# One chunk's x scaled ahead of a mask, one projection ordered by its low half, raw weights issued a round later, the last output tile in two halves

## The chip, the cores and the metric

The kernel runs on one core of a Trainium2 chip. The metric is the device time of one execution in microseconds (us). The core has five engines that work side by side and wait for one another through semaphores: TensorE (PE: matrix products; its weight loads are listed as PEld), VectorE (DVE), ScalarE (ACT), GpSimd (POOL) and SyncE (SP), which here only issues transfers. Each engine takes its instructions strictly in program order.

## The reference

Three layers follow one another. The first is attention with a decay: for each of 2 x 8 heads the 768 positions are taken in blocks of 64, and each block adds a masked product of its own q, k, v and a product with a running state of 64 x 64.

```python
for b in range(nb):                       # blocks of 64 positions
    intra = einsum('bhic,bhjc->bhij', qb, kb) * Dmask
    intra = einsum('bhij,bhjd->bhid', intra, vb)
    inter = einsum('bhid,bhde->bhie', qb * lam_pow, kv_state)
    out[:, :, sl] = intra + inter
    kv_state = lam_block * kv_state + einsum('bhsd,bhse->bhde', kb * rev_pow, vb)
```

Its output is x with 1536 tokens x 512 features. The second layer normalises each token (x divided by its root mean square, times a gain), forms silu(xn @ w_gate) * (xn @ w_val) with 1536 hidden features, and multiplies by w_out. The third takes the maximum of three products (768 features each) and multiplies by a last w_out. Activations are float32; the weights lie in memory as 64-bit floats.

## The kernel before, in words

**Numbers in two parts.** Every operand of the dense layers is held as a high half, rounded to the matrix engine's float32r, and a low half, the rest (names ending in h and l: xh, xl; wh, wl; hh, hl). A product is three matmuls: high x high, weight-high x operand-low, weight-low x operand-high (mm3, L467). A high half is made by ACT, its low half by POOL (DVE in a few places).

**Weights.** A unit is a 128 x 512 piece of a weight matrix. SP loads its raw 64-bit words (load_to, L152; three buffers). ACT takes two readings of the words (L238, L239), DVE does three steps (L196, L199, L202), POOL adds (L204); that gives float32 W. Then ACT rounds it to wh (L167) and POOL forms wl (L170). Three buffers of raw words mean that the load of raw unit n+3 waits until POOL's L204 of unit n is done.

**Attention.** The 1536 tokens are 12 chunks of 128. What one chunk needs is cut into pieces with one-letter names: T transposes k and q (L294, L296, copied to kT, qT by ACT), K scales the keys with the decay (kd, L284, POOL), C makes the scores and the state's products (sc, L318, L323), a and b apply the mask (A, L330, DVE; a also advances the state, S, L348), M mixes (px, L374) and reads px twice on ACT (squares sq, L385; x times the gain, L387), U sums the squares (pm on PE, ms on DVE, the power ri on POOL, L404), N spreads ri over a matrix (pb, L413), scales x with it on DVE (L415) and rounds it to xh on ACT (L417), R forms xl on POOL (L426). V finishes the state.

**The order of the work.** The table `orders` holds one string of letters for each round; in round s the letter T works on chunk s, C, a, b and V on s-1, M and U on s-2, N and R on s-3, K on s+1. This table is the order on every engine. Rounds 0 to 6 run ahead of the dense layers (the prologue, L972): in each, T of chunk s also asks for v of chunk s+1 and k, q of chunk s+2 (loads_to), then one raw unit is loaded (L987), and from round 2 on one unit is begun (begin_unit, L989: ACT's L238 and L239 go at the end of the round).

**Dense layers.** A block is 512 tokens, that is four chunks. The first stage's step 0 (hidden1, L605) makes pg = gate product, pv = value product of block 0: proj (L472) runs four slices of three matmuls each, and after every second slice gap() (L442) lets in the next pieces of attention and of weight making. The remaining attention pieces are spread over such gaps until about a quarter of the run. The last work is out2 (L847): twelve tiles of 128 tokens x 512 features, six matmuls each (L858 to L860), an addition on DVE (L865) and a store issued by SP (L868).

Of the kernel before, what the change touches and what calls it, by code (L numbers as in the profile page):

```python
# [12 lines left out]
ALU = mybir.AluOpType  # L13
# [5 lines left out]
P = 128  # L19
# [7 lines left out]
def tile_decay_attention_swiglu_maxout(  # L27
# [16 lines left out]
    nc = tc.nc  # L44
# [3 lines left out]
    KD = DM // P  # L48
    F1 = w_gate.shape[1] // P
    F2 = w1.shape[1] // P  # L50
    NB = 512
    HF = 2 * P
# [3 lines left out]
    NBLK = NT // NB  # L56
    CPB = S // P
    NCH = NT // P
    CPNB = NB // P
# [11 lines left out]
    def bank(name):  # L71
        return psum.tile([P, 512], F32, tag="bank", name=name)
# [70 lines left out]
    units = {}  # L143
# [6 lines left out]
    pos = {"load": 0, "made": 0, "raw": 0, "step": 0, "gap": 0, "quiet": False, "lag": 3, "narrow": True, "seam": False}  # L150

    def load_to(n):  # L152
        while pos["load"] < min(n, len(raw_list)):
            nm, f = raw_list[pos["load"]]
            t = wp.tile([P, KD, 2 * P], I32, tag="raw", name="wraw", bufs=3)
            for to, src in crosswise(t, source[nm](f)) if nm in "gv" else [(t, source[nm](f))]:
                nc.sync.dma_start(out=to, in_=src)
            raws[nm, f] = t
            pos["load"] += 1
# [260 lines left out]
    def rest(c):  # L420
# [7 lines left out]
    named = dict(M=(2, mixed), N=(3, normed), C=(1, scores), a=(1, masked(0)), R=(3, rest),  # L428
                 b=(1, masked(1)), U=(2, summed), V=(1, advance), T=(0, lambda c: (loads_to(c + 2), turn(c))),
                 K=(-1, decayed_keys))  # L430
    orders = ["MCaNbTURVK"] * (CPNB + 2) + ["MCaNRbTUVK"] + ["MNCRaUbVTK"] * NCH
    attn_q = [(s_, named[ch][1], s_ - named[ch][0]) for s_ in range(NCH + 3) for ch in orders[s_]
              if (ch == "K") <= s_ - named[ch][0] < NCH]
    gaps = [0, 0]
# [32 lines left out]
    def mm3(out, wh, wl, xh_, xl_, first, last):  # L467
        nc.tensor.matmul(out=out, lhsT=wh, rhs=xh_, start=first, stop=False)  # L468
        nc.tensor.matmul(out=out, lhsT=wh, rhs=xl_, start=False, stop=False)  # L469
        nc.tensor.matmul(out=out, lhsT=wl, rhs=xh_, start=False, stop=last)  # L470

    def proj(ps, unit, bh, bl):  # L472
        wh, wl = unit
        for kk in range(KD):
            ks = slice(kk * P, (kk + 1) * P)
            mm3(ps, wh[:, ks], wl[:, ks], bh[:, kk, :], bl[:, kk, :], kk == 0, kk == KD - 1)
            if kk % 2:
                gap()

    def split(dst_h, dst_l, src):  # L480
# [124 lines left out]
    def hidden1(f, j):  # L605
        bh, bl = x_block(j)
        pg = bank("pg")
        proj(pg, units["g", f], bh, bl)
        pv = bank("pv")
        proj(pv, units["v", f], bh, bl)  # L610
        if j == NBLK - 1:
            free(("g", f), ("v", f))
        sg = act.tile([P, NB], F32, tag="sg", name="sg", bufs=1)
        nc.scalar.activation(out=sg, in_=pg, func=AF.Silu)
        nc.vector.tensor_tensor(out=sg, in0=pv, in1=sg, op=ALU.mult)  # L615
        return sg
# [43 lines left out]
    def free(*keys):  # L660
        for key in keys:
            del units[key]
            room[held.pop(key)] += 1
# [183 lines left out]
    def out2(g, j, t):  # L847
        last = g == F2 // 2 - 1
        if g == 0 and t == 0:
            acc_sb[j] = act.tile([P, KD, NB], F32, tag="acc", name="acc_sb", bufs=3)  # L850
        ts = slice(t * P, (t + 1) * P)
        acc = bank("acc")
        for d in range(2):
            while ("p", 2 * g + d) not in units:
                third_of_unit()
            wh, wl = units["p", 2 * g + d]
            hh, hl = parts[j, d]
            nc.tensor.matmul(out=acc, lhsT=hh[:, ts], rhs=wh, start=d == 0, stop=False)  # L858
            nc.tensor.matmul(out=acc, lhsT=hh[:, ts], rhs=wl, start=False, stop=False)  # L859
            nc.tensor.matmul(out=acc, lhsT=hl[:, ts], rhs=wh, start=False, stop=d == 1)  # L860
        y = acc_sb[j][:, t, :]
        if g == 0:
            nc.scalar.copy(out=y, in_=acc)
        else:
            nc.vector.tensor_tensor(out=y, in0=acc, in1=y, op=ALU.add)  # L865
        if last:
            r0 = j * NB + t * P
            nc.sync.dma_start(out=out[r0:r0 + P, :], in_=y)  # L868
        if (j, t) == (NBLK - 1, NB // P - 1):
            free(("p", 2 * g), ("p", 2 * g + 1))  # L870
        gap()
        if t % 2 and g < 2:
            third_of_unit()
# [70 lines left out]
    with tc.manual_schedule():  # L944
        nc.scalar.dma_start(out=lam8, in_=lam.rearrange("(o h) -> o h", o=1).to_broadcast([P, H]))
        loads_to(0)
        for to, src in crosswise(g_sb, rms_g.rearrange("(a p) -> p a", p=P)):
            nc.scalar.dma_start(out=to, in_=src)
        make_identity(nc, ident)
        nc.vector.memset(ones, 1.0)  # L950
        nc.vector.memset(zeros, 0.0)
        nc.scalar.activation(out=mhalf, in_=zeros[:, 0:1], func=AF.Silu)
        nc.vector.memset(mhalf, -0.5)
        warm = bank("warm")
        for i in range(9):
            nc.tensor.matmul(out=warm[:, 0:P], lhsT=zeros, rhs=zeros, start=True, stop=True)
        nc.vector.tensor_tensor(out=diag, in0=ident[:, :C], in1=ident[:, C:], op=ALU.add)
        for h in range(H):
            nc.vector.tensor_tensor_scan(
                out=Tm[:, h, :], data0=lam8[:, h:h + 1].to_broadcast([P, C]), data1=diag,  # L960
                initial=0.0, op0=ALU.mult, op1=ALU.add)
        for hf in range(2):
            nc.vector.tensor_copy(out=lamh[64 * hf:64 * hf + 64, :],
                                  in_=lam8.rearrange("p (a t) -> p t a", t=2)[64 * hf:64 * hf + 64, hf, :])
        for a in range(NP):
            nc.vector.tensor_tensor_scan(
                out=lami[:, a, :], data0=lamh[:, a:a + 1].to_broadcast([P, C]), data1=zeros[:, :C],
                initial=1.0, op0=ALU.mult, op1=ALU.add)
        loads_to(1)
        pos["narrow"] = False  # L970
        unit_ = None
        for s_ in range(CPNB + 3):  # L972
            if stage1:
                unit_ = stage1.pop(0)
            while attn_q[0][0] == s_:
                fn = attn_q[0][1]
                attn_step()
                if unit_ and fn is named["b"][1]:
                    words_of_unit(0, *unit_)
                elif unit_ and fn is named["U"][1]:  # L980
                    words_of_unit(1, *unit_)
                    if stage2:
                        finish_unit(*stage2.pop(0))
                elif unit_ and fn is named["V"][1]:
                    words_of_unit(2, *unit_)
                    stage2.append(unit_[:3])
            load_to(pos["load"] + 1)  # L987
            if s_ > 1:
                begin_unit()  # L989
        pos["narrow"] = True  # L990
        finish = first_stage()
        pos["step"] = len(steps)
        second_stage(finish)
# [31 lines left out]
```

## Time and profile before

| | |
|---|---|
| median of 3 runs | 547.83 us (547.78 to 549.16) |
| the profiled execution | 550.31 us, its span 548.5 us |
| PE busy | 529.8 us (97% of the span) |
| DVE, ACT, POOL busy | 376.5, 278.6, 316.3 us |
| PE over the span's 40 slices | 7697979999... then 99% to the end |
| the last chain of waits, by engine | PE 85%, POOL 4%, issue 3%, DVE 3%, SP's queue 2%, ACT 2% |

The span is the time from the first to the last instruction; 550.31 - 548.5 = 1.8 us lie around it. A digit of the PE row is the busy share of 13.7 us in tenths. So PE has unfilled time only in the first seven or eight slices, some 100 us, in which attention, the making of weights and the first dense steps share the engines. "issue" in a row means that an engine waited for nothing that the profile shows. In a row of the time line the first number is the start, the second the time that the instructions took, and a bracket at the end is the idle time ahead of it and what ended that.

### The profile page before, as it was taken

How to read it: one execution, taken by the hardware profiler on the slowest of the kernel's cores; microseconds unless marked ns; L12 is line 12 of the kernel's file. 1: busy time of each engine (PE TensorE's matmuls, PEld its weight loads, DVE VectorE, ACT ScalarE, POOL GpSimd, SP SyncE). 2: the span in 40 equal slices, each digit the busy share in tenths (PEclk: the TensorE clock that was granted, in tenths of full speed). 3: DMA queues.
4: the chain of work that ended last, by engine and by line, in shares of the span. 5: the costliest groups of instructions: out<-in, count | busy, mean ns of one | idle time of the engine just before them, and what ended most of it. 6: DMA issues, size and time to landing. Idle time of an engine off the chain costs nothing.

```text
span 548.5 us, 9716 instructions
## 1 busy us (share of the span) xinstructions
PE 529.8 (97%) x3722; PEld 438.9 (80%) x3722; DVE 376.5 (69%) x663; ACT 278.6 (51%) x541; POOL 316.3 (58%) x251
## 2 busy tenths in 40 slices
PE   7697979999999999999999999999999999999997
PEld 7685858878888888888888888888888888888885
DVE  6688995447795666657776686877777477684464
ACT  3576754344556665255446426556466755651120
POOL 2469996212899557165455736986387554962050
PEclk9978999999999999999999999999999999999999
DMA  8987566000212222121221312121123222300014
GB/s 193 231 195 185 140 179 155 2 3 0 78 34 82 78 67 86 39 76 39 78 76 39 115 39 77 40 76 38 40 78 114 82 76 75 83 33 0 0 55 176
DMA packets 65454, 44.67 MB, mean 81 GB/s; under 512 B 40064, under 2 KB 61568, under 8 KB 65408
## 3 DMA queue, kind: packets, MB, share of 16 engines
q1 hardware_dynamic: 64704, 44.05, 28.3%
q8 instruction: 29, 0.48, 0.4%
q14 instruction: 17, 0.14, 0.1%
q10 hardware_dynamic: 704, 0.01, 0.1%
HBM read 40.90 MB, written 3.15 MB: 80 GB/s over the span
## 4 chain that ended last, share of the span: by engine, by line
PE 85%; POOL 4%; issue 3%; DVE 3%; SPq 2%; ACT 2%; DMA 1%; POOLq 0%; ACTq 0%
PE p L676 34%; PE r L676 8%; PE acc L468 6%; PE acc L470 6%; PE acc L469 6%; PE q L676 4%; PE acc L859 3%; PE acc L858 3%; PE acc L860 3%; PE pv L468 2%; PE pv L469 2%; PE pv L470 2%; PE pg L468 2%; SPq L92 2%; PE pg L470 2%
## 5 line engine op out<-in xcount | busy, mean ns | idle before, releaser
L170 POOL TENSOR_TENSOR wl<-W,wh 128x512 fp32r<-128x512 f32 x77 | 105.6, 1371 | 39.4 <-ACT wh L167 39.2
L204 POOL TENSOR_TENSOR W<-W,wraw 128x512 int32<-128x512 int32 x60 | 81.3, 1356 | 79.3 <-DVE W L202 70.8
L167 ACT CAST wh<-W 128x512 fp32r<-128x512 f32 x77 | 47.8, 621 | 85.3 <-POOL W L204 84.9
L482 POOL TENSOR_TENSOR hl<-sg,hh 128x512 fp32r<-128x512 f32 x36 | 48.5, 1348 | 25.7 <-ACT hh L481 25.7
L676 PE MATMUL p<-xh,wh 128*128 128x512 f32 x148 | 57.6, 389 | 0.0
L676 PE MATMUL p<-xl,wh 128*128 128x512 f32 x148 | 57.6, 389 | 0.0
L676 PE MATMUL p<-xh,wl 128*128 128x512 f32 x148 | 57.6, 389 | 0.0
L468 PE MATMUL acc<-hh,wh 128*128 128x512 f32 x144 | 56.5, 393 | 0.0
L469 PE MATMUL acc<-hl,wh 128*128 128x512 f32 x144 | 56.1, 389 | 0.0
L470 PE MATMUL acc<-hh,wl 128*128 128x512 f32 x144 | 56.1, 389 | 0.0
L831 DVE TENSOR_TENSOR acc_sb<-acc,acc_sb 128x512 f32<-128x512 f32 x46 | 31.8, 691 | 21.6 <-PE acc L470 20.6
L238 ACT ACTIVATE W<-wraw 128x512 f32<-128x512 f32 x60 | 40.2, 670 | 6.8 <-DMA wraw<-in_moe_w_dram 4.3
L481 ACT CAST hh<-sg 128x512 fp32r<-128x512 f32 x36 | 22.3, 620 | 35.0 <-DVE sg L615 26.4
L239 ACT ACTIVATE wraw<-wraw 128x512 int32<-128x512 uint32 x60 | 39.7, 662 | 0.0
L731 ACT COPY c<-p 128x512 f32<-128x512 f32 x34 | 20.0, 588 | 38.1 <-PE p L676 38.0
L482 POOL TENSOR_TENSOR hl<-m,hh 128x512 fp32r<-128x512 f32 x18 | 24.0, 1343 | 23.0 <-ACT hh L481 22.9
L196 DVE TENSOR_SCALAR mid<-W 128x512 f32<-128x512 f32 x50 | 34.2, 685 | 3.0 <-ACT W L238 3.0
L199 DVE TENSOR_SCALAR mid<-mid 128x512 int32<-128x512 int32 x50 | 34.7, 694 | 0.7
L676 PE MATMUL p<-yh,wh 128*128 128x512 f32 x90 | 35.0, 389 | 0.0
L676 PE MATMUL p<-yl,wh 128*128 128x512 f32 x90 | 35.0, 389 | 0.0
L676 PE MATMUL p<-yh,wl 128*128 128x512 f32 x90 | 35.0, 389 | 0.0
L202 DVE SCALAR_TENSOR_TENSOR W<-wraw,mid 128x512 int32<-128x512 int32 x50 | 34.0, 680 | 1.0
(175 smaller groups left out, 1349.1 us busy)
## 6 DMA issues: line engine op xcount, KB each, us to landing
wraw<-in_moe_w_out_dram SPq DMA_DIRECT2D x18, 512.0 KB, 3.4
wraw<-in_moe_w_dram SPq DMA_DIRECT2D x18, 512.0 KB, 3.6
kn<-in_k_dram SPq DMA_DIRECT2D x12, 256.0 KB, 4.3
qn<-in_q_dram SPq DMA_DIRECT2D x12, 256.0 KB, 5.3
vn<-in_v_dram SPq DMA_DIRECT2D x12, 256.0 KB, 4.2
wraw<-in_moe_w_gate_dram SPq DMA_DIRECT2D x12, 256.0 KB, 3.0
wraw<-in_moe_w_gate_dram SPq DMA_DIRECT2D x24, 128.0 KB, 3.6
wraw<-in_moe_w_val_dram SPq DMA_DIRECT2D x12, 256.0 KB, 3.0
```

Of the source, the lines that this page charges most:

```text
L167: nc.scalar.copy(out=wh, in_=W.bitcast(F32))
L170: nc.gpsimd.tensor_tensor(out=wl, in0=W.bitcast(F32), in1=wh.bitcast(F32), op=ALU.subtract)
L196: nc.vector.tensor_scalar(out=mid[key].bitcast(F32), in0=W.bitcast(F32), scalar1=LEAST, scalar2=MOST, op0=ALU.max, op1=ALU.min)
L199: nc.vector.tensor_scalar(out=mid[key], in0=mid[key], scalar1=0x07FFFFFF, scalar2=3, op0=ALU.bitwise_and, op1=ALU.logical_shift_left)
L204: nc.gpsimd.tensor_tensor(out=W, in0=W, in1=lo, op=ALU.add)
L238: nc.scalar.activation(out=W.bitcast(F32), in_=hi.bitcast(F32), func=AF.Abs)
L239: nc.scalar.activation(out=lo, in_=lo.bitcast(U32), func=AF.Copy, scale=2.0 ** -29)
L468: nc.tensor.matmul(out=out, lhsT=wh, rhs=xh_, start=first, stop=False)
L469: nc.tensor.matmul(out=out, lhsT=wh, rhs=xl_, start=False, stop=False)
L470: nc.tensor.matmul(out=out, lhsT=wl, rhs=xh_, start=False, stop=last)
L482: nc.gpsimd.tensor_tensor(out=dst_l, in0=src, in1=dst_h.bitcast(F32), op=ALU.subtract)
L676: nc.tensor.matmul(out=ps, lhsT=w[:, ks], rhs=r[:, o + k, :], start=first and k == 0 and n == 0, stop=k == 1 and n == 2, skip_group_check= ...
```

## The change

It has four parts. (1) In round 6 the order "MCaNRbTUVK" becomes "MCNRabTUVK": N of chunk 3 stands ahead of the mask a of chunk 5. (2) In step 0 the gate projection orders its twelve matmuls so that the eight that read xh come first and the four that read xl last; the gaps stay after the sixth and the twelfth. (3) No raw unit is loaded in round 0, so each of the prologue's raw loads is issued one round later. (4) The last of the twelve output tiles is computed as two halves of 256 columns, each in a bank of its own, with an addition and a store each.

On DVE, round 6 before and then after (x<-x,pb is L415 of chunk 3; A<-sc the two masks of chunk 5; W<-wraw,mid a step of weight making):

```order
49 L202 SCALAR_TENSOR_TENSOR W<-wraw,mid 128x512
50 L330 TENSOR_TENSOR A<-sc_826,Tm 128x4x64
51 L348 SCALAR_TENSOR_TENSOR S<-S,lami,sc_826 128x64 x4
52 L415 TENSOR_TENSOR x<-x,pb 128x512
53 L330 TENSOR_TENSOR A<-sc_827,Tm 128x4x64
54 L196 TENSOR_SCALAR mid<-W 128x512
```

```order
49 L202 SCALAR_TENSOR_TENSOR W<-wraw,mid 128x512
50 L415 TENSOR_TENSOR x<-x,pb 128x512
51 L330 TENSOR_TENSOR A<-sc_824,Tm 128x4x64
52 L348 SCALAR_TENSOR_TENSOR S<-S,lami,sc_824 128x64 x4
53 L330 TENSOR_TENSOR A<-sc_825,Tm 128x4x64
54 L196 TENSOR_SCALAR mid<-W 128x512
```

The scaling of x moves over one mask and four state instructions. No row of ACT or POOL moves against its neighbours.

On PE, the first half of the gate projection in step 0, before and then after (pg is its bank; px the mixing of chunk 5 in the first gap):

```order
353 L400 MATMUL pm<-ones,sq 128x1 x4
354 L468 MATMUL pg<-xh,wh 128x512
355 L469 MATMUL pg<-xl,wh 128x512
356 L470 MATMUL pg<-xh,wl 128x512
357 L468 MATMUL pg<-xh,wh 128x512
358 L469 MATMUL pg<-xl,wh 128x512
359 L470 MATMUL pg<-xh,wl 128x512
360 L374 MATMUL px_932<-qs,S 64x64
```

```order
353 L400 MATMUL pm<-ones,sq 128x1 x4
354 L478 MATMUL pg<-xh,wh 128x512
355 L478 MATMUL pg<-xh,wl 128x512
356 L478 MATMUL pg<-xh,wh 128x512
357 L478 MATMUL pg<-xh,wl 128x512
358 L478 MATMUL pg<-xh,wh 128x512
359 L478 MATMUL pg<-xh,wl 128x512
360 L374 MATMUL px_928<-qs,S 64x64
```

All readers of xl now stand behind the first gap, as the last four of the twelve.

On SP, the difference at the head of its queue (kn, qn, vn are loads of k, q, v; wraw a raw unit; rows with + are new there):

```order
+L92 DMA kn<-in_k_dram 128x8x64
+L92 DMA qn<-in_q_dram 128x8x64
+L92 DMA vn<-in_v_dram 128x8x64
 L92 DMA kn<-in_k_dram 128x8x64
 L92 DMA qn<-in_q_dram 128x8x64
```

```order
 L157 DMA wraw<-in_moe_w_out_dram 128x1024
-L92 DMA vn<-in_v_dram 128x8x64
-L92 DMA kn<-in_k_dram 128x8x64
-L92 DMA qn<-in_q_dram 128x8x64
 L157 DMA wraw<-in_moe_w_gate_dram 128x2x256
```

Three loads of 256 KB now go ahead of each of the first six raw units; behind the sixth the two orders agree again.

```diff
--- before.py
+++ after.py
@@ -428,7 +428,7 @@
     named = dict(M=(2, mixed), N=(3, normed), C=(1, scores), a=(1, masked(0)), R=(3, rest),
                  b=(1, masked(1)), U=(2, summed), V=(1, advance), T=(0, lambda c: (loads_to(c + 2), turn(c))),
                  K=(-1, decayed_keys))
-    orders = ["MCaNbTURVK"] * (CPNB + 2) + ["MCaNRbTUVK"] + ["MNCRaUbVTK"] * NCH
+    orders = ["MCaNbTURVK"] * (CPNB + 2) + ["MCNRabTUVK"] + ["MNCRaUbVTK"] * NCH
     attn_q = [(s_, named[ch][1], s_ - named[ch][0]) for s_ in range(NCH + 3) for ch in orders[s_]
               if (ch == "K") <= s_ - named[ch][0] < NCH]
     gaps = [0, 0]
@@ -469,12 +469,15 @@
         nc.tensor.matmul(out=out, lhsT=wh, rhs=xl_, start=False, stop=False)
         nc.tensor.matmul(out=out, lhsT=wl, rhs=xh_, start=False, stop=last)
 
-    def proj(ps, unit, bh, bl):
+    def proj(ps, unit, bh, bl, early=False):
         wh, wl = unit
-        for kk in range(KD):
-            ks = slice(kk * P, (kk + 1) * P)
-            mm3(ps, wh[:, ks], wl[:, ks], bh[:, kk, :], bl[:, kk, :], kk == 0, kk == KD - 1)
-            if kk % 2:
+        todo = [(kk, w, x) for kk in range(KD) for w, x in ((wh, bh), (wh, bl), (wl, bh))]
+        if early:
+            todo.sort(key=lambda e: e[2] is bl)
+        for n, (kk, w, x) in enumerate(todo):
+            nc.tensor.matmul(out=ps, lhsT=w[:, kk * P:(kk + 1) * P], rhs=x[:, kk, :], start=n == 0,
+                             stop=n == len(todo) - 1)
+            if n % 6 == 5:
                 gap()
 
     def split(dst_h, dst_l, src):
@@ -605,7 +608,7 @@
     def hidden1(f, j):
         bh, bl = x_block(j)
         pg = bank("pg")
-        proj(pg, units["g", f], bh, bl)
+        proj(pg, units["g", f], bh, bl, early=pos["step"] == 0)
         pv = bank("pv")
         proj(pv, units["v", f], bh, bl)
         if j == NBLK - 1:
@@ -850,22 +853,27 @@
             acc_sb[j] = act.tile([P, KD, NB], F32, tag="acc", name="acc_sb", bufs=3)
         ts = slice(t * P, (t + 1) * P)
         acc = bank("acc")
+        todo = []
         for d in range(2):
             while ("p", 2 * g + d) not in units:
                 third_of_unit()
             wh, wl = units["p", 2 * g + d]
             hh, hl = parts[j, d]
-            nc.tensor.matmul(out=acc, lhsT=hh[:, ts], rhs=wh, start=d == 0, stop=False)
-            nc.tensor.matmul(out=acc, lhsT=hh[:, ts], rhs=wl, start=False, stop=False)
-            nc.tensor.matmul(out=acc, lhsT=hl[:, ts], rhs=wh, start=False, stop=d == 1)
+            todo.extend(((hh, wh), (hh, wl), (hl, wh)))
         y = acc_sb[j][:, t, :]
-        if g == 0:
-            nc.scalar.copy(out=y, in_=acc)
-        else:
-            nc.vector.tensor_tensor(out=y, in0=acc, in1=y, op=ALU.add)
-        if last:
-            r0 = j * NB + t * P
-            nc.sync.dma_start(out=out[r0:r0 + P, :], in_=y)
+        r0 = j * NB + t * P
+        ends = last and (j, t) == (NBLK - 1, NB // P - 1)
+        for cs in (slice(0, HF), slice(HF, NB)) if ends else (slice(0, NB),):
+            if cs.start:
+                acc = bank("acc")
+            for n, (x, w) in enumerate(todo):
+                nc.tensor.matmul(out=acc[:, cs], lhsT=x[:, ts], rhs=w[:, cs], start=n == 0, stop=n == len(todo) - 1)
+            if g == 0:
+                nc.scalar.copy(out=y, in_=acc)
+            else:
+                nc.vector.tensor_tensor(out=y[:, cs], in0=acc[:, cs], in1=y[:, cs], op=ALU.add)
+            if last:
+                nc.sync.dma_start(out=out[r0:r0 + P, cs], in_=y[:, cs])
         if (j, t) == (NBLK - 1, NB // P - 1):
             free(("p", 2 * g), ("p", 2 * g + 1))
         gap()
@@ -984,7 +992,8 @@
                 elif unit_ and fn is named["V"][1]:
                     words_of_unit(2, *unit_)
                     stage2.append(unit_[:3])
-            load_to(pos["load"] + 1)
+            if s_:
+                load_to(pos["load"] + 1)
             if s_ > 1:
                 begin_unit()
         pos["narrow"] = True
```

## Rows read from the trace of the kernel before

**Rows 1.** Time line of PE, 18 to 80 us: instructions behind an idle time.

```profile
18.60 0.34 PE L323 MATMUL sc<-vn,kd 64*64 64x64 f32 x8 [1.24 <-issue]
...
25.92 0.69 PE L323 MATMUL sc<-vn,kd 64*64 64x64 f32 x29 [2.62 <-issue]
...
42.52 0.50 PE L468 MATMUL pg<-xh,wh 128*128 128x512 f32 x1 [1.01 <-ACT xh L417]
...
44.76 0.79 PE L469 MATMUL pg<-xl,wh 128*128 128x512 f32 x1 [1.74 <-POOL xl L426]
...
70.52 0.46 PE L374 MATMUL px<-qs,S 64*64 64x64 f32 x16 [0.94 <-DVE S L348]
...
75.97 0.32 PE L318 MATMUL sc<-qT,kT 64*64 64x64 f32 x2 [2.14 <-ACT x L387]
...
79.92 0.38 PE L400 MATMUL pm<-ones,ss 128*128 128x1 f32 x2 [0.70 <-ACT sg L614]
```

**Rows 2.** Time line of POOL, 38 to 48 us: four of its instructions.

```profile
38.18 0.55 POOL L404 TENSOR_TENSOR ri<-ms,mhalf 128x1 f32<-128x1 f32 x1 [1.91 <-DVE ms L402]
...
41.17 1.30 POOL L204 TENSOR_TENSOR W<-W,wraw 128x512 int32<-128x512 int32 x1
...
43.43 1.27 POOL L426 TENSOR_TENSOR xl<-x,xh 128x512 fp32r<-128x512 f32 x1
...
46.41 1.47 POOL L204 TENSOR_TENSOR W<-W,wraw 128x512 int32<-128x512 int32 x1
```

**Rows 3.** Time line of ACT, 15 to 48 us: four that waited.

```profile
15.60 0.67 ACT L238 ACTIVATE W<-wraw 128x512 f32<-128x512 f32 x1 [0.59 <-DMA wraw<-in_moe_w_gate_dram]
...
20.86 0.62 ACT L417 CAST xh<-x 128x512 fp32r<-128x512 f32 x1 [2.45 <-DVE x L415]
...
41.85 0.62 ACT L417 CAST xh<-x 128x512 fp32r<-128x512 f32 x1 [1.32 <-DVE x L415]
...
47.91 0.62 ACT L167 CAST wh<-W 128x512 fp32r<-128x512 f32 x1 [2.84 <-POOL W L204]
```

**Rows 4.** Time line of DVE, 39 to 44 us.

```profile
39.98 0.42 DVE L330 TENSOR_TENSOR A<-sc,Tm 128x256 f32<-128x256 f32 x1
...
41.08 0.68 DVE L415 TENSOR_TENSOR x<-x,pb 128x512 f32<-128x512 f32 x1
...
43.47 0.42 DVE L303 TENSOR_TENSOR qs<-pq,lami 128x256 f32<-128x256 f32 x1 [0.78 <-ACT qT L300]
```

**Rows 5.** Time line of SP: issues of loads, 9 to 15 us.

```profile
9.00 3.10 SPq L157 DMA_DIRECT2D wraw<-in_moe_w_gate_dram  x3
12.15 0.60 SPq L92 DMA_DIRECT2D vn<-in_v_dram  x1
...
15.21 2.98 SPq L157 DMA_DIRECT2D wraw<-in_moe_w_val_dram  x3
```

**Rows 6.** The page's engines and instruction queue (packets, MB, share); then 22.8 to 23.0 us.

```profile
PE 529.8 (97%) x3722; PEld 438.9 (80%) x3722; DVE 376.5 (69%) x663; ACT 278.6 (51%) x541; POOL 316.3 (58%) x251
...
q8 instruction: 29, 0.48, 0.4%
...
q8 instruction: 1, 0.02, 51.9%
```

**Rows 7.** Stretches: length, busy PE PEld DVE ACT POOL, granted clock, DMA share, GB/s.

```profile
27.00:31.00 4.00, 3.89 (x53) 3.69 (x51) 3.22 (x11) 2.49 (x5) 0.62 (x2) 0.54 0.74 186
31.00:34.00 3.00, 3.00 (x97) 2.88 (x98) 2.00 (x7) 2.45 (x8) 3.00 (x4) 0.50 1.05 250
```

**Rows 8.** The end: additions of the last tiles, a weight load elsewhere, the stores' landing.

```profile
543.61 0.69 DVE L865 TENSOR_TENSOR acc_sb<-acc,acc_sb 128x512 f32<-128x512 f32 x1 [0.67 <-PE acc L860]
544.97 0.69 DVE L865 TENSOR_TENSOR acc_sb<-acc,acc_sb 128x512 f32<-128x512 f32 x1 [0.67 <-PE acc L860]
...
14.06 0.97 PEld L400 LDWEIGHTS pm<-ones,sq 128*128 128x128 f32 x8
...
DMA to landing us min/median/max: 2.0/2.0/2.0
```

## The prediction

> **What bounds the kernel now.** I read the busy shares first, then PE's time line for what it waits for, then POOL, ACT and DVE around those waits. PE is busy 97% of the span [rows 6], so only the early part can give anything, and there I ask which engine ends each wait. PE has three kinds of idle time. Twice it stops in the middle of a run of equal matmuls, for 1.24 and 2.62 us, and the releaser is "issue", not a semaphore [rows 1]. At the start of step 0 it waits 1.01 us for xh of chunk 3 (ACT) and 1.74 us for its xl (POOL) [rows 1]. Between 70 and 80 us it waits 0.94 us for DVE, 2.14 and 0.70 us for ACT, 3.78 us in all [rows 1]; after 79.92 no wait of this size is left, and PE alone sets the end.
>
> The last group decides. From 38.18 us POOL works without a gap: ri, wl, xl, W (41.17), kd, xl (43.43), ri, wl, W (46.41); only the first row has a bracket [rows 2]. ACT, in order, stands 2.84 us until 47.91 for that W [rows 3], and the squares of chunk 5 are queued behind it; DVE's work on x comes behind those. So from 38 to 80 us a chain POOL, ACT, DVE carries the time, and PE meets it again at 70.5, 76.0 and 79.9. What PE gains between 42 and 70 us is lost at these waits unless the chain comes earlier too.
>
> **The change part by part.**
>
> N ahead of mask a. In round 6 the scaling of x starts at 41.08, behind the mask that starts at 39.98 and four state instructions [rows 4]; its matmul pb is done before. Moved in front it starts at 39.98, 1.10 us sooner. ACT is idle from 41.85 - 1.32 = 40.53 [rows 3], so xh is begun at about 40.7, not 41.85. PE's wait for it, 1.01 us, goes: PE came to it at 42.52 - 1.01 = 41.51 [rows 1], and its own work before that is late next. The mask and the state come 0.68 us later, but the products that read them run only in the first gap. On DVE the copy-dependent qs at 43.47 waited 0.78 us for ACT [rows 4]; ACT is about a microsecond ahead, so DVE's following work comes some 0.7 us sooner.
>
> Low half last. xl of chunk 3 comes from POOL at 43.43 + 1.27 = 44.70. POOL's order does not change and it has no gap since 38.18 [rows 2], so this time stands. Six matmuls that read xh now run ahead of it, about 1.4 us at 0.23 us each, then chunk 5's mixing in the gap; by then xl is there. PE's wait of 1.74 us goes. No instruction is added. Together PE is 1.01 + 1.74 = 2.75 us ahead at the end of the first projection. What is worth of that at the end: nothing, since ri, wl, W on POOL and all that ACT and DVE do behind them start when they did; the waits at 70 to 80 us grow from 3.78 us by the lead. Bounds for this term: 2.75 us gained (chain not binding), and 0.5 us lost or gained in it, because DVE's earlier work meets other POOL instructions: POOL's W took 1.47 us at 46.41 against 1.30 at 41.17 [rows 2], 0.17 us for each of about three such instructions. I take a gain of 0.2 us, near the lower end, since POOL's row at 46.41 has DVE beside it before and after.
>
> Raws a round later. Each of the first six raw units now stands behind three more loads of 256 KB. Before, raw unit 0 was issued at 9.00 and ACT waited for it, 0.59 us, until 15.60 [rows 3, 5]. The three loads took from 12.15 to 15.21, 3.06 us, to issue [rows 5], so unit 0 is 3.1 us later: ACT's reading at about 18.7. Queued behind it on ACT are the squares and x of chunk 1, then xh of chunk 0, before which ACT stood idle 2.45 us, until 20.86 [rows 3]. That cover takes 2.45 of 3.1; 0.6 us remain, on kT and qT of chunk 3 and so on PE's scores of chunk 3. They are hidden as long as PE stops 2.62 us, until 25.92, in those scores [rows 1]; without that stop they cost 0.6 us. k, q and v come about 3 us sooner, but no wait of PE in these rows is for them, so nothing is gained. From unit 3 on a raw load must wait for POOL's W three units back in either order, and k, q, v no longer queue behind that wait. I take 0, with ends of +0.6 (or what the next paragraph gives).
>
> The two stops. PE runs 2 x 3722 instructions, and a queue named instruction moved 29 packets in the span [rows 6]: one for about 257. The stops come one round apart, in the same product of the scores, and a packet of that queue started between 22.8 and 23.0 us [rows 6], 3 us before PE went on. I read the stops as waits for PE's own instructions behind a full load queue. [...] Whether the new order makes them shorter or longer the rows don't tell: bytes asked for by 27 us are about equal, in another sequence. I take 0. Ends: both stops gone, 3.86 us; a further one like the larger, 2.62 us more. [...]
>
> The last tile. Two additions start 544.97 - 543.61 = 1.36 us apart, so six matmuls of 512 columns take 1.36 us, 0.227 each [rows 8]. Twelve of 256 columns take 1.36 us again if the time goes by columns; if each also pays a weight load, 0.97 / 8 = 0.12 us [rows 8], it is 12 x 0.235 = 2.8 us. These loads overlap the matmul before, and 0.12 us is just about the half matmul's 0.113, so I take 0.12 each: 1.44 us, 0.08 more. The last addition is 0.42 (the mask of 256 columns [rows 4]), not 0.69 us [rows 8]: 0.27 less; the first half's is done before. The store landed in 2.0 us twelve times out of twelve [rows 8]; half the bytes could save 1.0 at most, I take 0, as no row shows a smaller store. Sum -0.2 us (ends -1.3 and +1.2).
>
> **Sum.** 550.31 us of the profiled execution (548.5 us span, 1.8 around it): -0.2 (first projection) -0.2 (tail) + 0 (loads) = 549.9. The three runs' median is 547.83, 2.5 us below the profiled one; the same -0.4 gives 547.4 us.
>
> **The rivals.**
>
> The lead is kept. If POOL's chain has slack that the rows hide, PE's 2.75 us arrive at the end, and the tail's 0.2: 544.9 us. For it: PE's waits are the ones the change removes. Against: ACT's 2.84 us for POOL's W, and the waits at 70 to 80.
>
> [...]
>
> Slower: a third stop. k, q, v of later rounds no longer wait behind raw units, so the load queue stays full past 27 us, where GB/s had fallen to 186 [rows 7]. The instruction packet for the next border, near 32 us, is then late: 1.2 to 2.6 us, all ahead of POOL's 38.18, 549 to 550.4, about 549.8 with the tail. It decides once that packet starts some 4 us after the border before it, as at 22.8.
>
> The split tile paying its weight loads in full is within the forecast's range (+1.2).
>
> **How the numbers follow.** Forecast 0.52, its own range 546.3 to 548.9; lead kept 0.10; prologue shortens 0.20; third stop 0.18. A measurement of this kernel tells about 0.3% from no change, 1.6 us: faster is below 546.2, slower above 549.5. Faster: 0.09 of the forecast's, 0.10 and 0.19, together 0.38. Slower: 0.01 and 0.14, 0.15. Same: 0.47. Left out below 544.0 is some half of the prologue's case, above 550.0 about half of the third stop's, so 544.0 to 550.0 us.
>
> **What would show it.** Right: PE's waits at step 0 gone, POOL still without a gap from about 38 us on and its ri near 38.2, PE's waits at 70 to 80 us grown to 5 to 6.5 us, PE free of waits from 80 us on as before; ACT's first reading of raw words about 3 us later; the last twelve matmuls 1.4 to 1.5 us. Wrong: POOL's ri of chunk 3 more than 1 us from 38.2, stops of PE at "issue" that went or came, or PE's waits at 70 to 80 not grown.

## The result

The change made the kernel slower: the median of seven runs is 550.28 us (549.65 to 551.79), against 547.78 us (546.64 to 549.16) of seven runs of the kernel before on the same chip, a ratio of 1.0053 with a 95% interval of 1.0036 to 1.0071. That is outside the range of 544.0 to 550.0 us by 0.28 us, on the side that had a chance of 0.15. The sum for the profiled execution, 549.9, looks met by the one profiled now (549.65 us, span 547.9), but only by accident: the one read before was 2.5 us above its kernel's median, the one now is the fastest of its seven.

### The profile page after: what moved, and what is told of

The parts are those of the page before. It is cut to its first block, busy times and chain, and to the rows that moved or that the text cites. A ratio compares the mean times of both kernels' runs of the same rounds, so it can differ in the third digit from the quotient of the medians.

```text
span 547.9 us, 9730 instructions
## 1 busy us (share of the span) xinstructions
PE 532.3 (97%) x3728; PEld 440.2 (80%) x3728; DVE 374.7 (68%) x664; ACT 278.9 (51%) x541; POOL 316.1 (58%) x251
## 4 chain that ended last, share of the span: by engine, by line
PE 85%; DMA 3%; POOL 3%; issue 3%; DVE 3%; ACT 2%; SPq 1%; ACTq 0%; POOLq 0%; DVEq 0%
PE p L679 34%; PE acc L870 9%; PE r L679 8%; PE acc L468 6%; PE acc L469 6%; PE acc L470 6%; PE pv L478 5%; PE pg L478 5%; PE q L679 4%; DMA kn<-in_k_dram 3%; PE px L374 1%; SPq L92 1%; POOL W L204 1%; DMA vn<-in_v_dram 1%; POOL wl L170 1%
## 5 line engine op out<-in xcount | busy, mean ns | idle before, releaser
L238 ACT ACTIVATE W<-wraw 128x512 f32<-128x512 f32 x60 | 40.1, 668 | 11.0 <-DMA wraw<-in_moe_w_gate_dram 4.1
L239 ACT ACTIVATE wraw<-wraw 128x512 int32<-128x512 uint32 x60 | 39.8, 664 | 0.0
```

What stands on the lines that cost most here:

```text
L238: nc.scalar.activation(out=W.bitcast(F32), in_=hi.bitcast(F32), func=AF.Abs)
L239: nc.scalar.activation(out=lo, in_=lo.bitcast(U32), func=AF.Copy, scale=2.0 ** -29)
```

## The profile after

PE's time line after the change, its idle times between 17 and 80 us, against [rows 1] (start, length, engine, line, operation, tiles, shapes, count, and in brackets the idle time ahead and what ended it):

```profile
17.82 0.34 PE L323 MATMUL sc<-vn,kd 64*64 64x64 f32 x8 [0.82 <-issue]
...
21.20 1.86 PE L400 MATMUL pm<-ones,sq 128*128 128x1 f32 x8 [1.75 <-ACT x L387]
...
40.89 0.72 PE L478 MATMUL pg<-xh,wh 128*128 128x512 f32 x1
...
51.23 0.38 PE L400 MATMUL pm<-ones,ss 128*128 128x1 f32 x2 [1.27 <-DVE ss L391]
...
60.08 0.69 PE L318 MATMUL sc<-qT,kT 64*64 64x64 f32 x32 [0.37 <-ACT qT L300]
...
70.36 0.46 PE L374 MATMUL px<-qs,S 64*64 64x64 f32 x16 [1.95 <-DVE S L348]
...
75.81 0.33 PE L318 MATMUL sc<-qT,kT 64*64 64x64 f32 x2 [0.64 <-ACT x L387]
...
79.73 0.38 PE L400 MATMUL pm<-ones,ss 128*128 128x1 f32 x2 [0.65 <-ACT sg L617]
```

Two things are gone: the stop of 2.62 us at "issue", and the waits of 1.01 and 1.74 us at step 0 (the row at 40.89 has no bracket). Two of more than 1 us are new: 1.75 us at 21.20, ahead of the column sums pm of chunk 1's squares, and 1.27 us at 51.23, where pm waits for DVE's ss. ACT (same columns) shows what stands ahead of the first, against [rows 3]:

```profile
18.85 0.69 ACT L238 ACTIVATE W<-wraw 128x512 f32<-128x512 f32 x1 [4.13 <-DMA wraw<-in_moe_w_gate_dram]
...
19.98 0.66 ACT L385 ACTIVATE sq<-px 128x256 f32<-128x256 f32 x2
20.50 1.16 ACT L387 ACTIVATE x<-px,g_sb 128x128 f32<-128x128 f32 x4
21.50 0.67 ACT L417 CAST xh<-x 128x512 fp32r<-128x512 f32 x1
...
24.79 0.68 ACT L238 ACTIVATE W<-wraw 128x512 f32<-128x512 f32 x1 [1.64 <-DMA wraw<-in_moe_w_val_dram]
...
47.82 0.62 ACT L167 CAST wh<-W 128x512 fp32r<-128x512 f32 x1 [3.56 <-POOL W L204]
```

ACT stands 4.13 us for raw unit 0 and reads it at 18.85, 3.25 us later than at 15.60; the squares stand behind that reading in ACT's order and end at 20.64. The squares are what pm reads, but its bracket names ACT's next instructions, x, and the times bear that out: the second of the four x ends at 21.14, 0.06 us ahead of pm. Both stand behind the reading. Why pm waits for that x is not shown; in the version with raws two rounds late, below, it starts right behind the first of the squares.

SP now issues the three raw loads of unit 0 from 12.56 us, 3.56 later than before, against [rows 5]:

```profile
12.56 2.21 SPq L157 DMA_DIRECT2D wraw<-in_moe_w_gate_dram  x3
```

TensorE's clock falls behind the new wait. The stretches after, against [rows 7] (length, busy PE PEld DVE ACT POOL with counts, granted clock, DMA share, GB/s):

```profile
20.00:24.00 4.00, 2.80 (x40) 2.72 (x40) 1.74 (x5) 3.15 (x10) 0.00 (x0) 0.56 1.01 260
24.00:27.00 3.00, 2.89 (x103) 2.66 (x96) 1.89 (x6) 2.21 (x7) 2.83 (x3) 0.50 0.94 245
27.00:31.00 4.00, 3.89 (x101) 3.63 (x97) 3.10 (x9) 2.62 (x8) 1.28 (x2) 0.96 0.82 208
```

It is 0.56 and 0.50 of full until 27 us. Before, it was 0.54 and 0.50 from 27 to 34 us, behind the stop of 2.62.

POOL after, against [rows 2]:

```profile
37.58 0.55 POOL L404 TENSOR_TENSOR ri<-ms,mhalf 128x1 f32<-128x1 f32 x1 [0.85 <-DVE ms L402]
...
40.57 1.30 POOL L204 TENSOR_TENSOR W<-W,wraw 128x512 int32<-128x512 int32 x1
...
42.84 1.29 POOL L426 TENSOR_TENSOR xl<-x,xh 128x512 fp32r<-128x512 f32 x1
...
46.03 1.76 POOL L204 TENSOR_TENSOR W<-W,wraw 128x512 int32<-128x512 int32 x1
```

The work is in the same order as before, from 37.58 in place of 38.18 us. The W that ACT waits for took 1.76 us in place of 1.47. The end, DVE's additions of the last two tiles, against [rows 8]:

```profile
543.37 1.14 DVE L874 TENSOR_TENSOR acc_sb<-acc,acc_sb 128x512 f32<-128x512 f32 x2 [0.67 <-PE acc L870]
544.80 0.42 DVE L874 TENSOR_TENSOR acc_sb<-acc,acc_sb 128x256 f32<-128x256 f32 x1 [0.29 <-PE acc L870]
```

From the addition of the tile before the last to the end of the last are 545.22 - 543.37 = 1.85 us, against 545.66 - 543.61 = 2.05 before: the 0.2 us of the prediction.

## The experiments

Each kernel was timed beside the kernel before on the same chip; three chips were used, so rows are compared by their ratios. The theory at the start: the late raw words cost the time, by way of ACT's order (reading, then chunk 1's squares, then PE's pm), and the other parts give nothing. The rivals: the two parts at step 0, or the split last tile, cost it, or the two measurements differ by the executions that they happened to meet.

| kernel | median us | ratio [95%] | ri of chunk 3 starts | span less that |
|---|---|---|---|---|
| before, once more | 547.45 | 0.9999 [0.9987, 1.0011] | 34.23 | 510.4 |
| after, once more | 549.64 | 1.0032 [1.0013, 1.0052] | 36.09 | 510.8 |
| only raws late | 549.55 | 1.0034 [1.0019, 1.0049] | 36.12 | 510.4 |
| after, raws as before | 546.95 | 0.9988 [0.9979, 0.9997] | 34.28 | 510.8 |
| only the two parts at step 0 | 547.05 | 0.9995 [0.9979, 1.0011] | 34.09 | 511.3 |
| only the split tile | 547.34 | 0.9996 [0.9980, 1.0012] | 34.79 | 510.6 |
| raws two rounds late | 552.32 | 1.0083 [1.0061, 1.0105] | 40.62 | 510.4 |
| after, first raw on time | 548.34 | 1.0016 [0.9996, 1.0036] | 34.95 | 512.8 |
| after, reading behind x | 548.76 | 1.0018 [1.0004, 1.0033] | 35.41 | 510.6 |
| the same, raws as before | 547.14 | 0.9990 [0.9973, 1.0007] | 35.19 | 510.3 |

The last two columns are of each kernel's profiled execution, the start being that of POOL's L404 as in [rows 2]. For the two executions told of above they are 38.18 and 510.3 (before), 37.58 and 510.3 (after).

**Both kernels once more.** Edit: none.

> The kernel before, unchanged, to see another of its executions. Theory A (the profiled execution of before, 550.3 us against a median of 547.8, had longer stops of TensorE at issue than most): a ratio of 1.000, and in a profile near 547.5 us the two stops (1.24 and 2.62 us) sum to under 2 us and the granted clock from 27 to 34 us is above 0.54, GpSimd's ri of chunk 3 starts at 35 to 36.5 us instead of 38.18. Theory B (the stops are the same in every execution, the changed kernel loses elsewhere): the stops are again 3.5 to 4 us in sum and ri starts within 0.5 us of 38.2.

> The changed kernel, unchanged, beside the parts below on one chip. Theory A (raw words a round late: +1.9 us by e1; x first, low half last, tail together: -0.7 us by e2): ratio 1.002 to 1.004. Theory C (the parts work against each other when together): 1.005 or more, as when it was first timed (1.0053).

The slowdown came again, 1.0032, with an interval that overlaps the first. The profile of the kernel before is the find. PE:

```profile
18.31 0.95 PE L400 MATMUL pm<-ones,sq 128*128 128x1 f32 x8
...
23.07 0.69 PE L323 MATMUL sc<-vn,kd 64*64 64x64 f32 x29 [1.54 <-issue]
...
38.57 0.51 PE L468 MATMUL pg<-xh,wh 128*128 128x512 f32 x1 [1.01 <-ACT xh L417]
...
40.80 0.80 PE L469 MATMUL pg<-xl,wh 128*128 128x512 f32 x1 [1.73 <-POOL xl L426]
...
66.56 0.46 PE L374 MATMUL px<-qs,S 64*64 64x64 f32 x16 [0.92 <-DVE S L348]
...
72.03 0.32 PE L318 MATMUL sc<-qT,kT 64*64 64x64 f32 x2 [2.17 <-ACT x L387]
...
75.96 0.38 PE L400 MATMUL pm<-ones,ss 128*128 128x1 f32 x2 [0.67 <-ACT sg L614]
```

Its stretches:

```profile
24.00:27.00 3.00, 2.89 (x78) 2.74 (x80) 2.50 (x8) 1.34 (x3) 1.82 (x2) 1.00 1.06 239
27.00:31.00 4.00, 3.56 (x99) 2.94 (x89) 3.72 (x13) 3.47 (x10) 2.88 (x3) 1.00 0.95 244
```

The waits from 38 us on are those of [rows 1] to within 0.03 us, each some 4 us earlier. Ahead of them there is one stop of 1.54 us in place of 1.24 and 2.62, and the clock stays at 1.00. This is the fastest of its eleven executions (546.35 us), but it is not alone: five profiles below have the raws and ACT's order as before (everything but the late raws, its two parts each alone, and both with a lighter POOL). In them ri of chunk 3 starts between 34.09 and 35.84 us, no stop between 15 and 38 us exceeds 1.55 us, and the clock is 1.00 from 24 to 38 us. So the stop of 2.62 us on which the prediction leaned, and the clock of 0.54 and 0.50 of [rows 7], belong to an execution, not to the kernel.

**Only the late raws.** Edit, on the kernel before:

```
-            load_to(pos["load"] + 1)
+            if s_:
+                load_to(pos["load"] + 1)
```

> Before, with only the raw loads a round later. Theory A (ScalarE waits for raw words with the squares of chunk 1 queued behind it, TensorE for the squares): 2.5 to 3 us slower than before, ratio 1.0045 to 1.006, ScalarE's first reading of raw words waits about 4 us for its load. Theory B (TensorE's lead out of the first projection costs its clock later, the raw loads do nothing): ratio within 0.999 to 1.001.

This alone gives the whole slowdown, 1.0034, if less than the 1.0045 to 1.006 that I expected. PE shows the same new wait:

```profile
20.79 1.05 PE L400 MATMUL pm<-ones,sq 128*128 128x1 f32 x8 [1.54 <-ACT x L387]
```

**Everything but the late raws.** Edit, on the kernel after:

```
-            if s_:
-                load_to(pos["load"] + 1)
+            load_to(pos["load"] + 1)
```

> The changed kernel with the raw loads put back where they were: x scaled ahead of the mask, low half last, last tile in halves remain. Theory A: the loss is gone, ratio 0.998 to 1.000 against before, and TensorE's waits at 70 to 80 us are grown by some 2 us while its end does not move. Theory B: still 2 to 2.5 us slower than before, ratio 1.004 to 1.005, with a granted clock under 0.8 between 70 and 75 us.

The slowdown is gone, and with 0.9988 [0.9979, 0.9997] this version is ahead of the kernel before too, if by only 0.1% and with an interval that just clears 1. The waits that I expected to grow at 70 to 80 us did not: PE waits 1.16 us at 67.08 and 2.13 us at 72.50.

**The two parts at step 0, and the split tile, each alone.** Edits, on the version above: `ends = False` (no split tile) for the one; for the other

```
-    orders = ["MCaNbTURVK"] * (CPNB + 2) + ["MCNRabTUVK"] + ["MNCRaUbVTK"] * NCH
+    orders = ["MCaNbTURVK"] * (CPNB + 2) + ["MCaNRbTUVK"] + ["MNCRaUbVTK"] * NCH
-        proj(pg, units["g", f], bh, bl, early=pos["step"] == 0)
+        proj(pg, units["g", f], bh, bl)
```

> Before, with x scaled ahead of the mask and the low half last; raw loads and last tile as before. Theory A (GpSimd, ScalarE and DVE carry the time from 35 to 76 us): ratio 0.9995 to 1.0005 against before, TensorE free of waits at the gate projection, but waiting for GpSimd's ri and for DVE's sum of squares within the next 10 us and at some 67 to 76 us as before; the sum of its waits from step 0 to 76 us within 1 us of the kernel before's (6.7 us by a profile of it). Theory of the lead kept: ratio 0.995, some 2.7 us.

> Before, with only the last output tile in two halves. From the changed kernel's last rows (twelve matmuls 0.12 us apart, last addition 0.42 us): 0.2 to 0.3 us faster at the end, ratio 0.9990 to 1.0005, no more than this measurement can tell; the last addition ends 1.85 to 1.9 us after the one before the last tile's, instead of 2.05.

Neither can be told from no change. What became of the lead of 2.75 us is seen in PE's idle times with the two parts at step 0:

```profile
41.48 0.49 PE L413 MATMUL pb<-ident,ri 128*128 128x128 f32 x2 [1.06 <-POOL ri L404]
...
47.75 0.38 PE L400 MATMUL pm<-ones,ss 128*128 128x1 f32 x2 [1.71 <-DVE ss L391]
...
56.59 0.69 PE L318 MATMUL sc<-qT,kT 64*64 64x64 f32 x32 [0.33 <-ACT qT L300]
...
66.86 0.46 PE L374 MATMUL px<-qs,S 64*64 64x64 f32 x16 [1.94 <-DVE S L348]
...
72.30 0.32 PE L318 MATMUL sc<-qT,kT 64*64 64x64 f32 x2 [2.13 <-ACT x L387]
```

Of 1.01 + 1.73 us that went, 1.06 + 1.71 came back by 48 us. DVE shows that its ss was not to be had sooner, first in the unchanged kernel, then here:

```profile
46.30 1.08 DVE L391 TENSOR_REDUCE ss<-sq 128x128 f32<-128x512 f32 x1 [0.62 <-ACT sq L385]
```

```profile
46.64 1.05 DVE L391 TENSOR_REDUCE ss<-sq 128x128 f32<-128x512 f32 x1 [3.51 <-ACT sq L385]
```

DVE now waits 3.51 us for ACT's squares, and ACT's wh ahead of those squares 4.11 us for POOL's W (3.56 us in the profile after, the row at 47.82 above). The lead meets POOL's chain within 8 us.

**Raws two rounds late.** Edit, on the kernel after: `if s_ > 1:`.

> The changed kernel with the raw loads one more round late (the first in round 2). Theory A: ScalarE's first wait grows by about 3 us to some 7 us, TensorE's for the squares behind it by as much; ratio 1.007 to 1.010 against before. If the lateness of the words is covered and only the order on the queue counts: 1.002 to 1.005, near the changed kernel.

The loss grows to 1.0083. PE waits 4.10 us at the same pm:

```profile
24.24 1.86 PE L400 MATMUL pm<-ones,sq 128*128 128x1 f32 x8 [4.10 <-ACT sq L385]
```

POOL's ri of chunk 3 is 6.4 us later than in the kernel before run again, and what follows it is as long as ever:

```profile
40.62 0.56 POOL L404 TENSOR_TENSOR ri<-ms,mhalf 128x1 f32<-128x1 f32 x1 [0.82 <-DVE ms L402]
```

**The first raw on time, the others late.** Edit, on the kernel after: `if s_ != 1:`.

> The changed kernel, but the first raw unit is loaded in round 0 as before (none in round 1, so all others stay a round late). Theory A with the first unit's wait as the main cost (ScalarE 3.7 to 4.1 us for it, TensorE 1.5 to 1.75 us for the squares behind it): ratio 0.998 to 1.001 against before, ScalarE's first wait under 1 us. If later units' lateness or the place of the loads on the queue cost the time: 1.003 and more, as the changed kernel.

Chunk 1's squares are free again; the next reading waits instead, and PE's wait behind it is 0.65 us, one round on:

```profile
23.65 0.67 ACT L238 ACTIVATE W<-wraw 128x512 f32<-128x512 f32 x1 [2.67 <-DMA wraw<-in_moe_w_val_dram]
```

1.0016 with an interval through 1 is unclear by itself and lies between the two expectations, and its profiled execution is out of line in the table (512.8): there the clock was at 0.50 from 75 to 80 us.

**The reading behind the squares.** Edit, on the kernel after: a unit is begun (ACT's L238 and L239) behind the next round's M, so behind squares and x, and no longer at the end of a round:

```
-            if stage1:
-                unit_ = stage1.pop(0)
...
+                if fn is mixed and s_ > 2:
+                    begin_unit()
+                    unit_ = stage1.pop(0)
...
-            if s_ > 1:
-                begin_unit()
+        begin_unit()
```

> The changed kernel, raw loads a round later, but ScalarE's two readings of a unit's raw words moved behind the squares and x of the next round's chunk; no other engine's order moves. Theory A with the queue behind ScalarE's wait as the cause: most of the loss is gone, ratio 0.998 to 1.002 against before, and TensorE has no wait near 21 us for ScalarE's x. If the raw loads harm by the order on the load queue or by instruction fetch instead: 2 to 3 us slower, ratio 1.004 to 1.006, as the changed kernel. Theory B: as the changed kernel.

PE's wait at pm is gone: it starts at 19.20, without a bracket. The loss is 1.0018 [1.0004, 1.0033], next to 1.0034 of the late raws alone on the same chip; the 0.8 us between the two medians are not clear of noise, and some loss stays. ACT:

```profile
19.04 0.68 ACT L238 ACTIVATE W<-wraw 128x512 f32<-128x512 f32 x1 [1.05 <-DMA wraw<-in_moe_w_gate_dram]
...
25.39 0.68 ACT L238 ACTIVATE W<-wraw 128x512 f32<-128x512 f32 x1 [1.99 <-DMA wraw<-in_moe_w_val_dram]
```

The readings come as late as in the kernel after, and xh, kT and qT now stand behind them. This was the direct test of ACT's order: only what queues behind the readings differs. In the trace PE's wait goes with the order; the medians show it in part at most. Where the rest of the loss lies is not shown: in this profile PE stops 0.73 and 1.65 us at "issue", and no other wait of PE between 11 and 40 us is above 0.27 us. That the new order is worth nothing by itself shows with the raws as before:

> The changed kernel with raw loads as before and ScalarE's two readings of raw words behind the next chunk's squares and x. Theory A: ScalarE's readings no longer hold up the squares, but xh, kT and qT now stand behind them: no more than 0.5 us either way against the version with only the raw loads put back, ratio 0.998 to 1.0005 against before. A rival, that the squares' place behind the readings also costs the kernel before a microsecond or two: ratio 0.995 to 0.997.

0.9990 [0.9973, 1.0007], like the version without it.

**POOL lightened.** Is POOL the carrier from 38 to 80 us, as the prediction said? Edit, on the kernel before and on the version with raws as before: the low halves of nine weight units of steps 0 to 3 are set to zero, 0.5 us each, in place of a subtraction of 1.3 to 1.5 us, so their part of the product is left out:

```
+            if pos["narrow"] and not lates and pos["step"] < 4:
+                nc.gpsimd.memset(wl.bitcast(I32), 0)
+            else:
...
```

> Before, with work left out on GpSimd: the low halves of nine weight units made in steps 0 to 3 are set to zero by a memset instead of being formed (1.3 to 1.8 us each). It asks whether GpSimd's chain carries the time after the prologue. Theory A: TensorE's waits at 66 to 76 us shrink, 3 to 5 us faster than before (TensorE's waits there sum to 3.9 us), ratio 0.991 to 0.995. Theory of TensorE as the bound from step 0 on: ratio 0.999 to 1.001.

> The same nine low halves set to zero by a memset (work left out), in the kernel with x ahead of the mask, low half last and last tile in halves, raw loads as before. Theory A: with GpSimd's chain shorter, TensorE's lead out of the first projection (2.75 us by its waits there) is no longer taken back in full: 1.5 to 3 us faster than the same kernel without the lead (the run above), where with the chain in place the gain was 0.5 us. Theory that the lead is lost elsewhere than at this chain (clock, DVE alone): 0 to 0.7 us faster than the run above.

Lighter POOL alone is worth 2.4 us, where I expected 3 to 5: 545.07 us, 0.9959 [0.9942, 0.9977]. PE's wait of 2.14 us for ACT's x at 76 us is gone; before S and sg it still waits 0.78 and 1.11 us. But the lead on top of it comes to 544.86 us, 0.9948 [0.9931, 0.9966], 0.2 us or 0.0011 better and not clear of noise, where I expected 1.5 to 3. That expectation failed. PE's waits with both:

```profile
48.80 0.38 PE L403 MATMUL pm<-ones,ss 128*128 128x1 f32 x2 [1.30 <-DVE ss L394]
...
67.97 0.46 PE L377 MATMUL px<-qs,S 64*64 64x64 f32 x16 [1.98 <-DVE S L351]
```

The first of them still has POOL behind it. DVE, ACT and POOL there:

```profile
47.71 1.03 DVE L394 TENSOR_REDUCE ss<-sq 128x128 f32<-128x512 f32 x1 [3.51 <-ACT sq L388]
...
45.39 0.62 ACT L167 CAST wh<-W 128x512 fp32r<-128x512 f32 x1 [4.14 <-POOL W L207]
...
46.31 0.53 POOL L171 MEMSET wl<- 128x512 int32 x1
```

DVE waits for ACT's squares, ACT ahead of them for POOL's W, and the first unit with its low half set to zero (46.31) comes only behind that W. So 1.30 us of the lead are lost before POOL is any lighter, and what a lighter POOL would be worth there was not tested. The second wait is for DVE, which is full (columns as above):

```profile
65.00:70.00 5.00, 2.92 (x72) 2.19 (x70) 4.96 (x9) 3.60 (x8) 4.40 (x5) 0.93 0.60 179
```

It is 1.98 us with the lead and 0.78 without, so 1.2 us of the lead end at DVE. The clock does not tell the two apart: from 38 to 80 us its mean is 0.92 in both profiles.

## Why the prediction was wrong

**The step that failed** is "Raws a round later ... I take 0", with an upper end of 0.6 us. Run alone, the part costs 0.0034 of the time, 1.9 us. The start of the working was right: it put ACT's reading at about 18.7, and it came at 18.85. One thing in the rest was wrong, and another stood on a single execution.

First, it counted ACT's idle time ahead of xh as the cover and did not price what stands between the reading and that idle time. The squares of chunk 1 stand there, and PE's pm reads them. The trace that I read had both ends of that gap. ACT in the kernel before:

```profile
16.75 0.64 ACT L385 ACTIVATE sq<-px 128x256 f32<-128x256 f32 x2
```

and PE in it:

```profile
20.08 0.95 PE L400 MATMUL pm<-ones,sq 128*128 128x1 f32 x8
```

The squares ended at 17.39, PE came to pm at 20.08: 2.69 us of slack, less than the 3.1 us by which the reading was put back. Of this slack 1.24 us was PE's own stop at 18.60; in the kernel before run again, which has no stop there, it is 18.31 - 16.92 = 1.39 us. After the change the squares end 20.64 - 17.39 = 3.25 us later, and PE, with a shorter stop of 0.82 us, comes to pm at 21.20 - 1.75 = 19.45, 0.63 us sooner. That makes 3.25 - 2.69 + 0.63 = 1.19 us of wait for the squares; the other 0.56 us, from 20.64 to 21.20, are those in which x runs. Measured: 1.75 us after, 1.71 in it run again, 1.54 with the late raws alone, 4.10 with them two rounds late.

Second, its cover was taken from one execution. What the prediction did price was right: it left 0.6 us on xh and what follows, and xh came 21.50 - 20.86 = 0.64 us later. The stop of 2.62 us that was to hide this is 1.54 us in the second execution of the kernel before, and in both profiles after there is no stop there. A stop that comes and goes can't be credited; but the loss came from the squares, not from here.

**What the wait then costs.** From pm's start to that of pb in round 3, PE took 27.01 - 21.20 = 5.81 us after, and 23.68 - 18.31 = 5.37 us in the kernel before run again, 1.54 of which was a stop: 3.83. So the half clock behind the wait cost 2.0 us. Wait, clock and the stop of 0.82, less the stop of 1.54 that did not come, are 3.0 us; ri of chunk 3 was 37.58 - 34.23 = 3.35 later. In the kernel after run again the clock fell later (0.50 from 24 to 27 us): pm to pb took 24.99 - 21.03 = 3.96 us, and ri was 36.09 - 34.23 = 1.86 later. These are single executions; the medians differ by 1.8 to 2.5 us.

**Prologue to the end.** A later or earlier ri of chunk 3 is kept to the end, as the table shows: over eleven of the twelve executions in which POOL's work is whole, the rest takes 510.3 to 511.3 us, while ri starts anywhere from 34.09 to 40.62. To within that 1 us, this case's loss lies ahead of it. By the prediction's own sign, ri near 38.2, the forecast looks right (37.58); that too is an accident, as ri stands at 34.09 to 35.84 in six of the seven profiles with the prologue of the kernel before. The sign against it that did show is the second stop, which went.

**The lead.** That the 2.75 us at step 0 are lost again was right, and the carrier too as far as the rows go (POOL's W, then ACT's wh, then the squares). The place was not: I looked for grown waits at 70 to 80 us, 5 to 6.5 in sum; after, they are 1.95 + 0.64 + 0.65 = 3.24. With the two parts alone the lead was gone by 48 us, and in the kernel after run again by 50 (1.07 + 1.70 us); in the first profile after 1.27 us of it were gone by 51, and the clock was at 0.75 from 38 to 44 us. POOL's chain also grew: from the start of ri to the end of the W at 46 us it took 47.79 - 37.58 = 10.21 us, against 47.88 - 38.18 = 9.70, the 0.5 us that the prediction had as a bound. Nor is POOL alone: from 65 us on DVE takes its part. How the loss divides between the two is open, as no run made DVE lighter, or POOL ahead of 46 us. The 0.2 us taken for the lead don't show: 0.9995 [0.9979, 1.0011].

**The tail.** Right in its parts: the halved matmuls start 0.12 us apart from 543.17 to 544.49, twelve of them, and the last addition takes 0.42. The halved stores, costed like the whole ones, came 0.2 us sooner, as the profile's transfers show (count, KB, median us to landing):

```profile
out_dram<-acc_sb SPq DMA_DIRECT2D x11, 256.0 KB, 2.0
out_dram<-acc_sb SPq DMA_DIRECT2D x2, 128.0 KB, 1.8
```

With some 0.4 us in all the part is too small to be told in a median (0.9996 [0.9980, 1.0012]).

**The rivals.** A lead that is kept is refuted. A prologue that shortens had a chance of 0.20 and set the lower end of 544.0 us. No run shows such a gain: with POOL's work whole the lowest ratio is 0.9988 (546.95 us). In six of the seven profiles with the prologue of the kernel before, ri of chunk 3 starts at 34.09 to 35.84 us already, with the clock at 1.00 from 24 to 38 us, so there was little left to give. "A third stop", at a border between the instructions of two packets, had the sign right and not the mechanism: the profile after has one stop, 0.82 us, and the slower side came from a wait of ACT for data, a queueing that I had listed and then priced at nothing. A third stop does exist, but with the raws as before: 0.77 us at 28.57 us in the version with everything but the late raws, 1.25 us at 28.78 us with the two parts alone.

**Open.** Why the stops at "issue" vary is not settled. In the kernel before they were 1.24 and 2.62, then only 1.54 us; after 0.82 and, run again, 0.73. The second stop is absent in all four profiles in which PE waits at pm of chunk 1 (after, twice; late raws alone; two rounds late), where PE comes there later. It is there with the late raws when PE does not wait ahead of it (1.65 us with the reading behind the squares, 1.55 with the first raw on time). So the wait seems to hide it, which was not tested by itself.

## What to carry to other kernels

When a load is issued later, follow the engine that reads it, in order: every instruction behind the reading is late, and each of its readers has its own slack, which must be larger than the delay; the idle time further down that engine covers only what stands behind it (here the squares came 3.25 us later, xh behind that idle time 0.64). Credit no cover that is a stop without a releaser (2.62 us in one execution here, 1.54 in another), and set a profiled execution that is above its kernel's median aside as one draw: here its prologue was 4 us longer than in another of the same kernel. An engine's lead is worth something only if the engines that feed it next come sooner too (here, with the two parts alone, 2.74 us of waits went at step 0 and 2.77 came back by 48 us). To test which of them takes it back, lighten that engine ahead of the place where the lead is lost; here the lighter units came too late for that.

## What I had not expected of the hardware

Behind PE's stop of 0.82 and wait of 1.75 us the granted clock was 0.56 and 0.50 until 27 us, and the same eight matmuls of pm took 1.86 us in place of 0.95. Run again, 0.73 and 1.71 us were followed by 0.95 and then 0.50, and pm took 1.05; a stop of 1.54 us in the kernel before left the clock at 1.00. So from pm to pb the wait of 1.75 us was followed by 2.0 us of loss, and that of 1.71 by 3.96 - 3.83 = 0.13.

The stops stand at the same instructions in several kernels, in the products of L323 after 24 and after 3 of 32 and in three versions in those of L318 after 15 of 32, and vary from nothing to 2.62 us. Between these places PE runs 125 and then 127 matmuls (17.32 to 22.84 and to 28.57 us in the version with everything but the late raws), each with a weight load: 250 and 254 instructions, near the 257 to a packet of the prediction. That the stops are waits for these packets was not tested.

Twelve matmuls of 256 columns, each with its own weight load, ran 0.12 us apart, little more than half of the 0.227 us that 512 columns take. Eight weight loads elsewhere took 0.97 us [rows 8], 0.12 each: at this size the loads still overlapped the matmuls (the one that starts at 543.29 us falls into the matmul from 543.17 to 543.45), and which of the two sets the pace can't be told.
